# VectorE's side work in attention, spread over five of the eight cycles of a group of heads

## The chip, the cores and the metric

The kernel runs on one core of a Trainium2 chip. Its time is device microseconds per execution, the median of three runs. Times inside an execution come from one profiled execution. The engines are TensorE (PE; its weight loads are PEld), VectorE (DVE), ScalarE (ACT), GpSimd (POOL) and SyncE (SP), which here only issues DMAs.

## The reference

For one sequence of 2048 tokens of width 448, two branches of the same input are mixed by a gate:

```
g = sigmoid((x * gate_w).sum(-1, keepdims=True))
a = attention(x)     # 16 heads of 28, one k and v for all; softmax(q k / sqrt(28)) v, then @ wo
b = x1 + gelu(layernorm(x1) @ w3) @ w4,   x1 = x + shifted(gelu(layernorm(x) @ w1)) @ w2
out = g * a + (1 - g) * b
```

All is computed in float32. The change lies in the attention.

## The kernel before

The projections, the token mixing and the MLP come first (to about 400 us); attention fills the rest. Each product that must be exact is made of three: a tensor is split into a high part, rounded to TensorE's format, and a low part, the rest, and high x high, high x low and low x high are added. The order of instructions on each engine is the order in which the code issues them; no scheduler moves any. Each engine takes its own in that order and waits on semaphores.

Attention runs over 16 groups u (`NU`): four blocks of 512 tokens times four groups of four heads. Within a group, the loop at line 895 makes eight **cycles** i = 0 to 7, each for two tiles of 128 keys. A cycle does this:

- TensorE makes the scores of the first key tile for four heads (`score_tiles`, L203), two heads into single banks, two into a pair of banks. ScalarE takes exponentials from the single banks (L855). VectorE copies the pair to SBUF (L903), and ScalarE takes its exponentials later from there; this spares ScalarE a wait on the banks.
- Then come the second tile's scores, with all exponentials by ScalarE from the banks.
- TensorE multiplies the values by the exponentials of the cycle before (`values`, L866) into a bank that the scores have left, and VectorE adds the result to the group's sum (`values_end`, L788 or L792). This is done in halves of 256 tokens, the first in `s0`, the second in `s1`.
- One **job** of the group before, a product with the output weights (`by_columns`, L818), goes into the other half of the first bank, once the first addition has read it; VectorE adds the result to the output (L837; for the last MLP products, which run as jobs in group 0, L849).

Cycles differ. At i = 2 (`MAX_AT`) the value product is made whole in one bank, and in place of a job TensorE makes a sample of the next group's scores (`max_part`, L210), whose maximum VectorE takes (L212). At i = 5 (`TWICE`) the value product is whole as well, and two jobs run. The jobs of a group are appended at i = 4 of the next one, so that group 0 runs the MLP's and group 1 has none until i = 4.

Beside this, VectorE has **side work**, issued right behind the L903 copy and ahead of `values_end`:

- i = 1: `recip` (L778, L804): the reciprocal of the sums of the group before, which is then sent to memory (`rd`) and read back to all partitions (`rb`, L808).
- i = 3: `max_end` (L236, L237, L240) of the next group, which `later` holds since i = 2: it negates the maximum, splits it and transposes it, and SP issues eight small DMAs (L244) that put it into spare rows of the next group's query `qh`, so that the scores come out with the maximum subtracted. Then `norm` (L813): the sums of the group before times `rb`. Group 0 has no `norm`; group 15 has no next maximum.
- i = 6: `q_begin` (L194, L195), which splits the query of the group after the next (`q_split`) into `qh` and `ql`. Then `q_fetch` has SP load the next raw query into the one buffer `qr` (L189, four DMAs). Groups 14 and 15 have none.

`qh` and `ql` have three buffers each. In group 0, `q_begin(1)` and a fetch stand at i = 1 as well.

Of the kernel before, what the change touches and what calls it, by code (L numbers as in the profile page):

```python
# [10 lines left out]
F32R = mybir.dt.float32r  # L11
# [5 lines left out]
P = 128  # L17
# [19 lines left out]
def f32(ap):  # L37
    return ap.bitcast(F32)
# [3 lines left out]
def gated_mix_kernel(  # L42
# [12 lines left out]
    nc = tc.nc  # L55
# [124 lines left out]
    NU = NB * NG  # L180
    kh_of = []
    qr_of, qh_of, ql_of = {}, {}, {}
# [5 lines left out]
        for j in range(4):  # L188
            nc.sync.dma_start(raw[32 * j:32 * j + DH], qd[g, DH * j:DH * j + DH, 512 * b:512 * b + 512])  # L189

    def q_split(u, qh, ql):
        qr = qr_of.pop(u)
        qh_of[u], ql_of[u] = qh, ql
        nc.vector.tensor_copy(qh, qr)  # L194
        nc.vector.tensor_sub(ql, qr, f32(qh))  # L195

    def scores(u, kt, ps):
        kh = kh_of[0]
# [450 lines left out]
    with tc.tile_pool(name="s2", bufs=1, reuse_waits="tile") as s2, \  # L649
# [36 lines left out]
        for b in range(NB):  # L686
            acc = [ps2.tile([P, 512], F32, tag="acc", bufs=4, name=f"acc_{b}_{t}") for t in range(4)]
            gs = {}
            for f in range(NF):
                if f == 9 and b + 1 < NB:  # L690
                    mv, rs = layernorm_stats(s2a, b + 1)
                if f == 10 and b + 1 < NB:
                    xt4 = big(f"xt4_{b + 1}")[:, 0:4 * D].rearrange("p (f t j) -> p f t j", f=NE, t=4)
                if f in (10, 11) and b + 1 < NB:
                    for t in (2 * f - 20, 2 * f - 19):
                        xn = s2a.tile([P, 512], F32, tag="xn", bufs=1, name=f"xn_{b + 1}_{t}")[:, 0:D]
                        layernorm_norm(b + 1, t, mv, rs, xn, xt4)
                if f == 11 and b + 1 < NB:
                    xt_write(b + 1, xt4)
                    ln_read(b + 1)  # L700
                gs[f] = w3_part(b, f)
                if b == 0 and f % 2 and f < 11:
                    split_w3((f + 3) // 2)
                    split_w4((f + 3) // 2)
                    if f < 9:
                        load_w34((f + 5) // 2, s2)
                if b == 1 and f == 0:
                    nc.gpsimd.tensor_tensor(gg, invE, gz, ALU.pow)
                    nc.vector.tensor_scalar(gg, gg, 1.0, None, op0=ALU.add)
                    nc.vector.reciprocal(gg, gg)  # L710
                    nc.vector.tensor_scalar(gi, gg, -1.0, 1.0, op0=ALU.mult, op1=ALU.add)
                if b == NB - 1 and f == 4:
                    weigh_x1(0, 4 * b)
                if b == 1 and f == 1:
                    nc.gpsimd.memset(f32(khd), 0.0)
                    for j in range(4):
                        h = slice(32 * j, 32 * j + DH)
                        nc.gpsimd.tensor_copy(khd[h, j * MK:(j + 1) * MK], f32(kh_of[0])[h, 0:MK])
                    qr0 = s2a.tile([P, 512], F32, tag="xn", bufs=1, name="qr_0")
                    nc.gpsimd.memset(qr0, 0.0)  # L720
                    q_load(0, qr0)
                    nc.sync.dma_start(w4_late, w4[F - P:F, :])
                if b == 1 and f == 5:
                    q_split(0, qh0, ql0)
                if f >= 2:
                    for t in range(4):
                        w4_part(f - 2, t, gs[f - 2], acc)
                        if b > 1 and t % 2 == 0 and f < NF - 1:
                            fill()
            for t in range(4):  # L730
                w4_part(NF - 2, t, gs[NF - 2], acc, NF - 2 if b == NB - 1 else NF - 1)
                if b + 1 < NB:
                    ln_split(b + 1, t, t + 1)
            for t in range(4):
                if b < NB - 1:
                    w4_part(NF - 1, t, gs[NF - 1], acc)
                xt = x1[:, 4 * b + t, :]
                nc.vector.tensor_add(xt, xt, acc[t][:, 0:D])  # L738
# [5 lines left out]
    with tc.tile_pool(name="s3", bufs=1, reuse_waits="tile") as s3, \  # L744
# [16 lines left out]
        def q_fetch(u):  # L761
            if u < NU:
                q_load(u, qr)

        def q_begin(u):
            q_split(u, s3.tile([P, 512], F32R, tag="qh", bufs=3, name=f"qh_{u}"),
                    s3.tile([P, 512], F32R, tag="ql", bufs=3, name=f"ql_{u}"))

        q_fetch(1)

# [40 lines left out]
        def norm(u, o, rb):  # L811
            on_of[u] = s3.tile([P, 512], F32, tag="on", bufs=2, name=f"on_{u}")
            nc.vector.tensor_mul(on_of[u], o, rb)  # L813
# [81 lines left out]
        for c in range(NC):  # L895
            u, i = divmod(c, NT // 2)
            k = 2 * c
            s0, s1, s2, s3_ = singles if c % 2 == 0 else singles[2:] + singles[:2]
            pa = score_tiles(u, 2 * i, s0, s1, pairs[0])
            exps(pa, left, s0.unsqueeze(1))  # L900
            exps(pa, right, s1.unsqueeze(1))
            if c < NC - 1:
                nc.vector.tensor_copy(pa[:, both], pairs[0])  # L903
            else:
                exps(pa, both, pairs[0])
            while later:
                later.pop(0)()
            if i == 1 and sums:
                norms.append(recip(*sums.pop()))
            if i == 1 and u == 0:  # L910
                q_begin(1)
                q_fetch(2)
            if i == 3 and norms:
                w = norms[0][0]
                norm(*norms.pop())
            if i == 6 and u + 2 < NU:
                q_begin(u + 2)
                q_fetch(u + 3)
            pb = score_tiles(u, 2 * i + 1, s2, s3_, pairs[1])
            exps(pb, left, s2.unsqueeze(1))  # L920
            exps(pb, right, s3_.unsqueeze(1))
            exps(pb, both, pairs[1])
            if c < NC - 1:
                exps(pa, both)
            if i == 4 and u:
                jobs += [(wo_products, wo_add, (u - 1, t), cols) for t in range(4) for cols in halves]
            if c == 0:
                run_jobs(s0, 2)
                run_jobs(s1, 2)
                continue  # L930
            v = (c - 1) // (NT // 2)
            most = 2 if i == TWICE or (u == NU - 1 and i > 3) else 1
            at_max = i == MAX_AT and u + 1 < NU
            if at_max or (most == 2 and jobs):
                values((k - 2, k - 1), s0)
                values_end(v, s0)
                if at_max:
                    max_part(u + 1, range(4), s1)
                    later.append(lambda u=u: max_end(u + 1))
                else:  # L940
                    run_jobs(s1, most)
            else:
                q0, q1 = slice(0, 256), slice(256, 512)
                values((k - 2, k - 1), s0[:, q0], q0)
                values_end(v, s0[:, q0], q0)
                values((k - 2, k - 1), s1[:, q0], q1)
                adds = job_products(s0[:, q1], 1)
                values_end(v, s1[:, q0], q1)
                job_adds(adds)
            if i == 0 and v < NU - 1:  # L950
                sums.append(sums_begin(v))
# [4 lines left out]
        u = NU - 1  # L956
# [84 lines left out]
        with tc.If(again > 0, label="redo"):  # L1041
            for b in range(NB):
                for g in range(NG):
                    u = b * NG + g
                    q_fetch(u)
                    q_begin(u)
                    max_full(u, bank)
                    max_end(u)
                    pv = banks.pop(0)
                    for kt in range(NT):  # L1050
                        ps = [bank(f"s2_{u}_{kt}_{j}") for j in range(4)]
                        scores(u, kt, ps)
                        p = s3.tile([P, 4, 512], F32, tag="p", bufs=PB, name=f"p2_{u}_{kt}")
                        for j in range(4):
                            exps(p, slice(j, j + 1), ps[j].unsqueeze(1))
                        for j in range(4):
                            nc.tensor.matmul(pv[32 * j:32 * j + 32, :], vext[:, kt, :], p[:, j],
                                             start=(kt == 0), stop=(kt == NT - 1), tile_position=(0, 32 * j))
                    values_end(u, pv)
                    banks.append(pv)  # L1060
                    norm(*recip(*sums_begin(u), False))
                    for t in range(4):
                        ps = bank(f"wo2_{u}_{t}")[:, whole]
                        wo_products(u, t, ps)
                        wo_add(u, t, ps)
# [51 lines left out]
```

## Time and profile before

| what | us |
|---|---|
| median of 3 runs (lowest to highest) | 944.64 (944.31 to 945.36) |
| the profiled execution, its own time | 944.86 |
| its span, first to last instruction | 943.1 |
| of that, before the first L903 copy | 403.5 |
| TensorE busy over the span | 928.3 |
| ScalarE busy over the span | 636.9 |
| VectorE busy over the span | 516.7 |

A line of a timeline has the start in us from the span's start, the length, the engine, the line of the code, the operation, what it writes and reads, how many instructions are merged in it, and in brackets how long its engine was idle before it and which instruction ended that. A line of the view by stretch has the bounds, the length, and for each engine the busy time with the number of instructions; then the granted TensorE clock, the DMA engines' share and GB/s. A matmul's end is modelled, so TensorE counted as busy can still be waiting in part. A row of waits has the total time, how often, and the longest.

### The profile page before, as it was taken

The numbers are of one execution on the slowest core, as the hardware profiler recorded it, in microseconds if no ns is written. First come the engines' busy times: TensorE is split into PE (matmuls) and PEld (weight loads), VectorE is DVE, ScalarE is ACT, GpSimd is POOL, SyncE is SP. The second block draws the span as 40 slices with busy tenths as digits, with TensorE's granted clock in tenths as the row PEclk, the third lists the DMA queues.
The fourth block names the chain that finished last, engine by engine and source line by source line (L and its number), as shares of the span: only waits on it lengthen the run. The fifth ranks groups of instructions, "written<-read, shape, count | busy, mean of one in ns | idle before, by whom it ended". The sixth has DMA issues, their size and how long they took to land.

```text
span 943.1 us, 22620 instructions
## 1 busy us (share of the span) xinstructions
PE 928.3 (98%) x9573; PEld 618.1 (66%) x9573; DVE 516.7 (55%) x922; ACT 636.9 (68%) x1006; POOL 81.1 (9%) x111
## 2 busy tenths in 40 slices
PE   9999999999999999999999999999999999999997
PEld 6788888888888888855555555555555555555552
DVE  3665264532432431166666666666666676666664
ACT  5542444332222221289999999999999999999993
POOL 3343420200000520020000000000000000000000
PEclk9999999999999999999999999999999999999998
DMA  9722652210300200020000011000011000010001
GB/s 315 280 76 56 168 164 89 55 48 1 84 1 1 84 1 0 1 62 22 14 15 24 14 42 34 23 13 16 24 43 33 15 23 13 27 41 17 10 14 42
DMA packets 40435, 47.24 MB, mean 50 GB/s; under 512 B 10120, under 2 KB 28488, under 8 KB 40328
## 3 DMA queue, kind: packets, MB, share of 16 engines
q1 hardware_dynamic: 37304, 40.27, 14.5%
q10 hardware_dynamic: 3024, 5.47, 1.6%
q8 instruction: 76, 1.25, 0.6%
q14 instruction: 31, 0.25, 0.1%
HBM read 32.56 MB, written 11.67 MB: 47 GB/s over the span
## 4 chain that ended last, share of the span: by engine, by line
PE 94%; ACT 3%; issue 1%; DMA 0%; DVE 0%; ACTq 0%; DVEq 0%
PE bank L866 25%; PE bank L203 19%; PE bank L818 6%; PE acc L682 5%; PE acc L684 5%; PE acc L683 5%; PE g L135 4%; PE g L136 4%; PE g L137 4%; ACT p L855 3%; PE pair L203 2%; PE hs L460 1%; PE hs L461 1%; PE g L138 1%; PE g L139 1%; PE h L135 1%
## 5 line engine op out<-in xcount | busy, mean ns | idle before, releaser
L855 ACT ACTIVATE p<-bank 128x512 f32<-128x512 f32 x512 | 265.1, 609 | 28.3 <-PE pair L203 18.1
L866 PE MATMUL bank<-p,vext 128*32 128x256 f32 (+1 forms) x3520 | 245.3, 415 | 4.7 <-ACT p L855 1.3
L866 PEld LDWEIGHTS bank<-p,vext 128*32 128x32 f32 x3520 | 101.4, 109 | 125.7 <-ACT p L855 57.5
L903 DVE COPY p<-pair 128x1024 f32<-128x1024 f32 x127 | 155.5, 1225 | 48.8 <-PE pair L203 39.1
L672 ACT ACTIVATE gh<-g 128x512 fp32r<-128x512 f32 x55 | 32.9, 598 | 184.6 <-PE g L139 184.6
L792 DVE TENSOR_TENSOR o<-o,bank 128x256 f32<-128x256 f32 (+1 forms) x188 | 88.1, 469 | 110.2 <-PE bank L866 99.6
L855 ACT ACTIVATE p<-p 128x1024 f32<-128x1024 f32 x127 | 139.5, 1098 | 0.0
L855 ACT ACTIVATE p<-pair 128x1024 f32<-128x1024 f32 x129 | 137.3, 1064 | 0.0
L674 DVE TENSOR_TENSOR gl<-gf,gh 128x512 fp32r<-128x512 f32 x55 | 38.3, 696 | 166.4 <-ACT gf L673 166.4
L203 PE MATMUL bank<-qh,kh 32*128 32x512 f32 x512 | 125.5, 450 | 0.0
L203 PE MATMUL pair<-qh,kh 32*128 32x512 f32 x512 | 118.1, 457 | 0.3 <-DVE x L738 0.3
L203 PE MATMUL bank<-ql,kh 32*128 32x512 f32 x512 | 111.0, 394 | 0.0
L203 PE MATMUL bank<-qh,kl 32*128 32x512 f32 x512 | 108.7, 389 | 0.0
L203 PE MATMUL pair<-qh,kl 32*128 32x512 f32 x512 | 101.0, 388 | 0.0
L203 PE MATMUL pair<-ql,kh 32*128 32x512 f32 x512 | 100.8, 389 | 0.0
L203 PEld LDWEIGHTS bank<-qh,kh 32*128 32x128 f32 x512 | 54.0, 182 | 62.3 <-issue 22.3
L682 PE MATMUL acc<-w4h,gh 128*128 128x448 f32 x220 | 80.3, 365 | 0.0
L684 PE MATMUL acc<-w4h,gl 128*128 128x448 f32 x220 | 80.0, 364 | 0.0
L683 PE MATMUL acc<-w4l,gh 128*128 128x448 f32 x220 | 80.0, 363 | 0.0
L818 PE MATMUL bank<-wof,on 128*32 128x224 f32 (+1 forms) x992 | 68.2, 362 | 0.2
L135 PE MATMUL g<-ah,w3h 128*128 128x512 f32 x168 | 65.8, 392 | 0.0
L136 PE MATMUL g<-al,w3h 128*128 128x512 f32 x168 | 65.7, 391 | 0.0
(199 smaller groups left out, 1416.8 us busy)
## 6 DMA issues: line engine op xcount, KB each, us to landing
qd<-qf ACTq DMA_DIRECT2D x16, 256.0 KB
rb<-rd SPq DMA_DIRECT2D x15, 256.0 KB
x<-in_x_dram SPq DMA_DIRECT2D x4, 896.0 KB
xd<-xt SPq DMA_DIRECT2D x16, 224.0 KB
w34raw<-in_w_dram SPq DMA_DIRECT2D x7, 512.0 KB
qr<-qd SPq DMA_DIRECT2D x64, 56.0 KB
out_dram<-ot SPq DMA_DIRECT2D x15, 224.0 KB
w34raw<-in_w_dram SPq DMA_DIRECT2D x7, 448.0 KB
```

The lines of the kernel that those rows point to most:

```text
L135: nc.tensor.matmul(ps, wh[:, c, :], ah[:, c, :], start=(c == 0), stop=False)
L136: nc.tensor.matmul(ps, wh[:, c, :], al[:, c, :], start=False, stop=False)
L203: nc.tensor.matmul(ps[j], k[h, keys], q[h, :], start=(r == 0), stop=(r == 2), tile_position=(32 * j, 0))
L674: nc.vector.tensor_sub(gl, gf, f32(gh))
L682: nc.tensor.matmul(ps, gh[:, tok], w4h[i][:, k, :], start=(f == 0), stop=False)
L683: nc.tensor.matmul(ps, gh[:, tok], w4l[i][:, k, :], start=False, stop=False)
L684: nc.tensor.matmul(ps, gl[:, tok], w4h[i][:, k, :], start=False, stop=(f == stop))
L792: nc.vector.tensor_add(o, o, pv)
L818: nc.tensor.matmul(ps[32 * i:32 * i + 32, :], a[:, c:c + 32], w, start=True, stop=True, tile_position=(0, 32 * i))
L855: nc.scalar.activation(p[:, heads], p[:, heads] if source is None else source, AF.Exp, scale=SCALE)
L866: nc.tensor.matmul(pv[32 * j:32 * j + 32, :], vext[:, kt, :], p_of[k][:, j, qs], start=(k == ks[0]), stop=(k == ks[-1]), tile_position=(0, ...
L903: nc.vector.tensor_copy(pa[:, both], pairs[0])
```

## The change

`q_split` becomes two functions: `q_high` makes the high part of the query, `q_low` the low part. In the loop the high part is made at i = 5 and the low part, with the fetch behind it, stays at i = 6. `max_end` is taken from `later` at i = 4 instead of at the first chance, which was i = 3. Where a split stood whole elsewhere (in the MLP, at i = 1 of group 0, and in the fallback that runs when a check of the sums fails) both functions are called one after the other. So the side work of a group, which stood in cycles 1, 3 and 6, stands in 1, 3, 4, 5 and 6. The number of instructions of each engine is the same, and so is the order on TensorE, ScalarE and GpSimd; VectorE's order changes, and on SP the DMAs of `max_end` move with it, in groups 4, 8 and 12 past the DMA of one output row.

```diff
-    def q_split(u, qh, ql):
-        qr = qr_of.pop(u)
+    def q_high(u, qh, ql):
         qh_of[u], ql_of[u] = qh, ql
-        nc.vector.tensor_copy(qh, qr)
-        nc.vector.tensor_sub(ql, qr, f32(qh))
+        nc.vector.tensor_copy(qh, qr_of[u])
+
+    def q_low(u):
+        nc.vector.tensor_sub(ql_of[u], qr_of.pop(u), f32(qh_of[u]))
...
         def q_begin(u):
-            q_split(u, s3.tile([P, 512], F32R, tag="qh", bufs=3, name=f"qh_{u}"),
-                    s3.tile([P, 512], F32R, tag="ql", bufs=3, name=f"ql_{u}"))
+            q_high(u, s3.tile([P, 512], F32R, tag="qh", bufs=3, name=f"qh_{u}"),
+                   s3.tile([P, 512], F32R, tag="ql", bufs=3, name=f"ql_{u}"))
...
-            while later:
+            if i == 4 and later:
                 later.pop(0)()
             if i == 1 and sums:
                 norms.append(recip(*sums.pop()))
             if i == 1 and u == 0:
                 q_begin(1)
+                q_low(1)
                 q_fetch(2)
             if i == 3 and norms:
                 w = norms[0][0]
                 norm(*norms.pop())
+            if i == 5 and u + 2 < NU:
+                q_begin(u + 2)
             if i == 6 and u + 2 < NU:
-                q_begin(u + 2)
+                q_low(u + 2)
                 q_fetch(u + 3)
```

More of the change, by code (lines that the diff above doesn't have):

```diff
@@ L723, in gated_mix_kernel @@
                 if b == 1 and f == 5:
-                    q_split(0, qh0, ql0)
+                    q_high(0, qh0, ql0)
+                    q_low(0)
                 if f >= 2:
@@ L1046, in gated_mix_kernel @@
                     q_begin(u)
+                    q_low(u)
                     max_full(u, bank)
```

## The prediction

> **What bounds the kernel now.** I read four views: the page for the whole run, the busy time of each engine by stretch, the waits of ScalarE, and the instructions in order of time, for one group after another. The page ends the question of a share of busy time at once: TensorE is busy nearly always, so the share alone says nothing of where a microsecond can be won.
>
> ```profile
> PE 928.3 (98%) x9573; PEld 618.1 (66%) x9573; DVE 516.7 (55%) x922; ACT 636.9 (68%) x1006; POOL 81.1 (9%) x111
> ```
>
> The change lies in attention alone. The second view gives 470 to 895 us, thirteen whole groups of heads (u = 2 to 14) of eight cycles each; the third gives ScalarE's waits in the same stretch (columns: total us, times, longest).
>
> ```profile
> 470.00:895.00 425.00, 421.76 (x6260) 222.77 (x6256) 284.64 (x504) 405.26 (x620) 0.00 (x0) 1.00 0.08 24
> ```
>
> ```profile
> ACT p L855 <- PE pair L203: 15.7, 47, 0.4
> ACT p L855 <- PE bank L203: 2.6, 8, 0.4
> ```
>
> ScalarE works 405.3 of 425.0 us and waits 18.3 us, 55 times, always for score products. That is just over four waits in each of 13 groups. Where they sit, the time order of ScalarE in group u = 6 shows (start, us, engine and line, idle before it in brackets); the first instruction of a cycle is the one on a bank:
>
> ```profile
> 611.36 2.06 ACT L855 ACTIVATE p<-bank 128x512 f32<-128x512 f32 x4 [0.23 <-PE pair L203]
> ...
> 615.67 2.07 ACT L855 ACTIVATE p<-bank 128x512 f32<-128x512 f32 x4 [0.39 <-PE pair L203]
> ...
> 623.94 2.06 ACT L855 ACTIVATE p<-bank 128x512 f32<-128x512 f32 x4 [0.40 <-PE pair L203]
> ...
> 628.20 2.06 ACT L855 ACTIVATE p<-bank 128x512 f32<-128x512 f32 x4 [0.34 <-PE bank L203]
> ```
>
> I name a cycle c0 to c7 by its i, and let it run from one L903 copy to the next. ScalarE's idle 0.39 us closes c3, 0.40 closes c5, 0.34 closes c6; the 0.23 behind c2 is not touched. 13 x (0.23 + 0.39 + 0.40 + 0.34) = 17.7 of the 18.3 us; the other 0.6 stand in three c1, where the reciprocal waited for its DMA:
>
> ```profile
> DVE good L778 <- DMA rt<-o: 2.0, 3, 0.7
> ```
> VectorE in the same cycles:
>
> ```profile
> 611.38 1.22 DVE L903 COPY p<-pair 128x1024 f32<-128x1024 f32 x1 [0.18 <-PE pair L203]
> 612.52 0.16 DVE L236 TENSOR_SCALAR mc<-mr 128x16 fp32r<-128x16 f32 x1
> ...
> 613.07 0.65 DVE L813 TENSOR_TENSOR on<-o,rb 128x512 f32<-128x512 f32 x1
> 613.63 0.42 DVE L792 TENSOR_TENSOR o<-o,bank 128x256 f32<-128x256 f32 x1
> ...
> 615.69 1.22 DVE L903 COPY p<-pair 128x1024 f32<-128x1024 f32 x1 [0.48 <-PE pair L203]
> 617.52 0.42 DVE L792 TENSOR_TENSOR o<-o,bank 128x256 f32<-128x256 f32 x1 [0.60 <-PE bank L866]
> ...
> 619.64 1.22 DVE L903 COPY p<-pair 128x1024 f32<-128x1024 f32 x1 [0.47 <-PE pair L203]
> 622.32 0.69 DVE L792 TENSOR_TENSOR o<-o,bank 128x512 f32<-128x512 f32 x1 [1.46 <-PE bank L866]
> ...
> 623.95 1.23 DVE L903 COPY p<-pair 128x1024 f32<-128x1024 f32 x1
> 625.10 0.42 DVE L194 CAST qh<-qr 128x512 fp32r<-128x512 f32 x1
> 625.55 0.69 DVE L195 TENSOR_TENSOR ql<-qr,qh 128x512 fp32r<-128x512 f32 x1
> 626.16 0.41 DVE L792 TENSOR_TENSOR o<-o,bank 128x256 f32<-128x256 f32 x1
> ...
> 628.22 1.23 DVE L903 COPY p<-pair 128x1024 f32<-128x1024 f32 x1 [0.48 <-PE bank L203]
> ```
>
> The reader is to see three lengths. c4, which has no side work, takes 615.69 to 619.64, 3.95 us, and in it VectorE idles 0.60 us ahead of the first L792 addition. c3 takes 4.31 us, c6 4.27 us, and in both VectorE goes from the copy through side work into L792 with no idle time. L792 frees the bank into which TensorE writes the next output product (L818), and behind that stand the scores of the next cycle, on which ScalarE waits. So **the loop of TensorE, VectorE and ScalarE** bounds the stage; side work costs time once it is longer than the cover of 0.60 us behind the copy.
>
> **How much of the two stalls is VectorE's.** Not all of it, and TensorE shows why. These rows are its value products in c3 and in c4:
>
> ```profile
> 612.15 1.93 PE L866 MATMUL bank<-p,vext 128*32 128x256 f32 x32
> ```
>
> ```profile
> 616.33 1.93 PE L866 MATMUL bank<-p,vext 128*32 128x256 f32 x32
> ```
>
> In c4 they start 0.64 us behind the copy, in c3 0.77 us: TensorE itself comes late out of c2, where the scores waited for the reduce. In c4 the first L792 follows 1.19 us (617.52 less 616.33) behind the value products; in c3 that would be 613.34, only 0.29 us ahead of the 613.63 measured. The cycle can't fall back to 3.95 us. Two cycles of the trace show what is left when side work is missing. In group u = 0 there is no norm, so c3 holds max_end alone; in group u = 14 there is no query to split, so c6 holds nothing:
>
> ```profile
> 416.17 1.22 DVE L903 COPY p<-pair 128x1024 f32<-128x1024 f32 x1 [0.18 <-PE pair L203]
> ...
> 418.15 0.42 DVE L792 TENSOR_TENSOR o<-o,bank 128x256 f32<-128x256 f32 x1 [0.22 <-PE bank L866]
> ...
> 420.26 1.22 DVE L903 COPY p<-pair 128x1024 f32<-128x1024 f32 x1 [0.46 <-PE pair L203]
> ```
>
> ```profile
> 887.09 1.23 DVE L903 COPY p<-pair 128x1024 f32<-128x1024 f32 x1
> 889.18 0.42 DVE L792 TENSOR_TENSOR o<-o,bank 128x256 f32<-128x256 f32 x1 [0.86 <-ACT p L855]
> ...
> 891.30 1.23 DVE L903 COPY p<-pair 128x1024 f32<-128x1024 f32 x1 [0.46 <-PE pair L203]
> ```
>
> So c3 is 4.09 us with 0.55 us of side work, VectorE then waiting 0.22 us for TensorE; c6 is 4.21 us with none.
>
> **The change part by part.**
>
> *max_end leaves c3.* Its three instructions fill 612.52 to 613.07, 0.55 us. The norm (0.65 us) then starts at 612.52 and ends at 613.17, ahead of the 613.34 at which TensorE lets the first L792 go. VectorE is no longer last, as in group 0, and c3 goes from 4.31 to 4.09: **0.22 us saved**. TensorE's late start is what is last then.
>
> *max_end enters c4.* The copy there begins at 615.69; the next instruction can start 1.14 us later (611.38 to 612.52), at 616.83, and 0.55 us of work ends at 617.38, ahead of the L792 at 617.52. The idle 0.60 us hides it with 0.14 us to spare: cost 0. Its input, the maximum of c2, is then a whole cycle old. With no cover it would cost 0.55 us in each group. Nothing else waits in line but L792, and L818 behind it.
>
> *The query's high half moves from c6 to c5.* It takes 0.42 us, and c5 has 1.46 us of idle time ahead of its only L792, since there all value products come first: cost 0, or 0.42 us without that cover. c5's own 0.40 us stays; it has two output products, and TensorE alone sets it. The raw query was loaded behind c6 of the group before, so no wait is added.
>
> *c6 keeps the low half.* 0.69 us from 625.10 ends at 625.79. In group 14 the first L792 came 2.09 us behind the copy, here 626.04, so VectorE isn't last: c6 goes from 4.27 towards 4.21, **0.06 us saved**.
>
> *The DMAs.* max_end issues eight small DMAs on SP, and with it they move one cycle back. The norm reads rb, and now starts 0.55 us earlier.
>
> ```profile
> 606.20 0.54 SPq L808 DMA_DIRECT2D rb<-rd  x1
> 613.21 4.56 SPq L244 DMA_DIRECT2D qh<-mrow  x8
> ```
>
> The issues would run from about 617.5 to 622.1. SP's next work, the loads of the next query, follows the low half, at 625.79 or later, so nothing queues behind them. In groups 4, 8 and 12 the output row of c3 is issued ahead of them instead of behind. The rows that they write are read by the next group's first scores, after c7's copy at 628.22, 6 us later. rb has been issued 5.8 us before the norm's new start. I cost both at 0.
>
> *How many groups.* c3 has both pieces and an output product in u = 2 to 14, 13 groups. In u = 1 the output products have not begun, and ScalarE opens c4 there with no idle time, so nothing is to be had:
>
> ```profile
> 451.30 1.12 ACT L855 ACTIVATE p<-bank 128x512 f32<-128x512 f32 x2
> ```
>
> c6 has the split and an output product in u = 1 to 13, 13 groups.
>
> **The sum.** 13 x 0.22 + 13 x 0.06 = 2.86 + 0.78 = 3.64 us, say 3.6. The profiled execution took 944.86 us (span 943.1 and 1.8 around it), which would be 941.3. It lies 0.2 above the median of the runs, 944.64; from that the forecast is **941.0 us**. Bounds of what the trace does not show: c4's margin of 0.14 us is small, and a loss of 0.05 in each of the 15 groups that have a max_end takes 0.8 back; the side work of c6 may cost all of its 0.06 still, 0.8 less; the 0.6 us of ScalarE's waits behind late reciprocals may go or double. That is 2.0 to 4.2 us, or 940.4 to 942.6, with 0.4 for the runs' own spread below.
>
> **The rivals.**
>
> *The stalls aren't VectorE's (no change, 944.6).* If TensorE's lag alone made c3 and c6 long, moving side work would do nothing. For it: the lag is real, and c6 without side work is only 0.06 us shorter. Against it: L792 has no idle time before it in c3 and has 0.22 us of it in group 0. [...] Chance 8%.
>
> *c4 pays in part (943.1).* If c3's extra 0.14 us in group 0 (4.09 less 3.95) were max_end's price and not the lag's, c4 would take it on in each of the 15 groups that have a max_end (u = 0 to 14): 15 x 0.14 = 2.1 us of the 3.6 given back. Against it is the 0.22 us of idle time behind max_end in group 0. Chance 5%.
>
> *Both stalls go whole (935.8).* c3 and c6 at 3.95 us would save 13 x (0.36 + 0.32) = 8.8 us. The two rows of groups 0 and 14 speak against it. Chance 4%.
>
> *Slower: max_end is exposed in c4 (949.2).* The first output product of a new set is issued in c4, behind L792. If there L792 could start as soon as VectorE is free, all 0.55 us would delay L792, L818, the scores and ScalarE: 15 x 0.55 = 8.2 us, less the 3.6 saved, is 4.6 us slower. It decides from a delay of 0.24 us in each c4 on, where cost and gain are equal (3.6 / 15); for that the cover of 0.60 us would have to shrink to some 0.3. It doesn't in c4 of group 6, where the copy before it is as long and TensorE's value products begin 0.64 us behind it. Chance 4%.
>
> **How the numbers follow.** Forecast 79%, no change 8%, c4 in part 5%, both whole 4%, slower 4%. Runs of this kernel tell 0.2% (1.9 us) from no change, so faster is below 942.75: forecast and both whole, 0.83; within 0.2%: no change and c4 in part, 0.13; slower 0.04. The range takes the forecast's bounds and the near end of the second rival: 940.0 to 942.9.
>
> **What would show it.** In the profile of the changed kernel the L903 copies should stand 4.09 us apart in c3, 3.95 in c4, 4.31 in c5 as before, 4.21 in c6; idle time of about 0.2 us ahead of L792 in c3 and c6 and about 0.1 in c4; ScalarE's idle time about 0.17 behind c3 and 0.29 behind c6, and its waits in the 13 groups about 14.7 us instead of 18.3. An L792 in c4 without idle time, or a copy there later than 3.95 us, would be the second or the last rival. A stall in front of the norm would show that rb lands later than I take it to.

## The result, and the profile after

The changed kernel takes **940.44 us** (median of 6 runs, 939.28 to 941.63), the kernel before 944.95 us beside it (6 runs, 942.69 to 945.37). The ratio is 0.9961, with an interval of 0.9951 to 0.9971; it is an estimate from all the runs, not the quotient of the two medians (0.9952), and is worth 3.7 us. On the 944.64 us of the prediction that is 940.96 us. The profiled execution of the changed kernel took 941.63 us; its span is 939.8 us, 3.3 us under that of before (3.23 by the unrounded times, which the sums below use).

First the page's line of busy times, and the view by stretch for the same thirteen groups (u = 2 to 14), which now end at 891.9 us:

```profile
PE 924.7 (98%) x9573; PEld 618.8 (66%) x9573; DVE 516.5 (55%) x922; ACT 637.4 (68%) x1006; POOL 81.6 (9%) x111
```

```profile
470.00:891.90 421.90, 418.65 (x6260) 223.66 (x6256) 284.39 (x504) 405.73 (x620) 0.00 (x0) 1.00 0.08 24
```

VectorE and ScalarE do the same work as before, to within 0.5 us; what went is waiting. TensorE's busy time falls from 421.76 to 418.65 us with the same 6260 matmuls, so part of what the profile counts as busy was waiting. ScalarE's waits in that stretch (total us, times, longest):

```profile
ACT p L857 <- PE pair L204: 11.0, 42, 0.5
ACT p L857 <- PE bank L204: 3.9, 13, 0.4
```

They sum to 14.9 us instead of 18.3, in as many places (55). Where they shrank, ScalarE's order of time in group 6 shows; these rows open c4 and c7, and the bracket is the idle time left by the cycle before:

```profile
614.35 2.06 ACT L857 ACTIVATE p<-bank 128x512 f32<-128x512 f32 x4 [0.17 <-PE bank L204]
...
626.83 2.06 ACT L857 ACTIVATE p<-bank 128x512 f32<-128x512 f32 x4 [0.30 <-PE pair L204]
```

Behind c3 0.17 instead of 0.39, behind c6 0.30 instead of 0.34; behind c2 and c5 the 0.23 and 0.39 us stand as they were. VectorE in the same group, c3 to c6:

```profile
610.28 1.23 DVE L905 COPY p<-pair 128x1024 f32<-128x1024 f32 x1 [0.17 <-PE bank L204]
611.42 0.68 DVE L815 TENSOR_TENSOR on<-o,rb 128x512 f32<-128x512 f32 x1
612.25 0.42 DVE L794 TENSOR_TENSOR o<-o,bank 128x256 f32<-128x256 f32 x1
...
614.37 1.22 DVE L905 COPY p<-pair 128x1024 f32<-128x1024 f32 x1 [0.46 <-PE bank L204]
...
615.92 0.21 DVE L241 STREAM_TRANSPOSE mrow<-mc 128x32 f32<-128x32 f32 x1
616.21 0.42 DVE L794 TENSOR_TENSOR o<-o,bank 128x256 f32<-128x256 f32 x1
...
618.32 1.22 DVE L905 COPY p<-pair 128x1024 f32<-128x1024 f32 x1 [0.46 <-PE pair L204]
619.46 0.42 DVE L193 CAST qh<-qr 128x512 fp32r<-128x512 f32 x1
621.00 0.69 DVE L794 TENSOR_TENSOR o<-o,bank 128x512 f32<-128x512 f32 x1 [1.12 <-ACT p L857]
...
622.63 1.22 DVE L905 COPY p<-pair 128x1024 f32<-128x1024 f32 x1
623.77 0.68 DVE L196 TENSOR_TENSOR ql<-qr,qh 128x512 fp32r<-128x512 f32 x1
624.72 0.42 DVE L794 TENSOR_TENSOR o<-o,bank 128x256 f32<-128x256 f32 x1 [0.27 <-ACT p L857]
...
626.85 1.23 DVE L905 COPY p<-pair 128x1024 f32<-128x1024 f32 x1 [0.46 <-PE pair L204]
```

From copy to copy: c3 614.37 less 610.28 is 4.09 us (4.31 before), c4 3.95 (3.95), c5 4.31 (4.31), c6 4.22 (4.27). In c3 and c6, where VectorE ran from the copy through its side work into the addition, it now idles 0.15 us (610.28 to 612.25: the norm ends at 612.10) and 0.27 us ahead of it. In c4 max_end ends at 616.13 and the addition starts at 616.21.

The copies of all groups, compared between the two profiles, divide the 3.23 us:

| where | us |
|---|---|
| c3 in u = 2 to 14 | -2.91 (0.224 each) |
| c6 in the 11 groups u = 2 to 13 other than 9 | -0.54 (0.049 each) |
| c5 and c6 of group 9 | +0.29 (+0.21 and +0.075) |
| c1 of group 0, where VectorE waits for the query's DMA | +0.38 |
| the other cycles (c6 of u = 1 is -0.045 of it) | -0.07 |
| ahead of the first copy, and behind attention | -0.34, -0.04 |

The part ahead of the first copy, which the change doesn't touch, took 401.25 to 403.7 us in the profiles of this study, and c1 of group 0 took 5.13 to 5.85 us. Each kernel was profiled once, so it isn't shown how much they differ between runs of one kernel; but the 45 runs of the kernel before in this study spread over 3.7 us (941.95 to 945.69), and these two parts would account for most of that. So below I read the spacing of copies inside attention first, and the time of the runs second.

### The profile page after: what moved, and what is told of

Same layout as the page of the kernel before. It is cut to its first block, busy times and chain, and to the rows that moved or that the text cites. A ratio compares the mean times of both kernels' runs of the same rounds, so it can differ in the third digit from the quotient of the medians.

```text
span 939.8 us, 22620 instructions
## 1 busy us (share of the span) xinstructions
PE 924.7 (98%) x9573; PEld 618.8 (66%) x9573; DVE 516.5 (55%) x922; ACT 637.4 (68%) x1006; POOL 81.6 (9%) x111
## 4 chain that ended last, share of the span: by engine, by line
PE 92%; ACT 4%; DMA 1%; issue 1%; DVE 1%; SPq 0%; POOL 0%; ACTq 0%; DVEq 0%
PE bank L868 24%; PE bank L204 18%; PE bank L820 5%; PE acc L683 5%; PE acc L685 5%; PE acc L684 5%; ACT p L857 4%; PE g L135 4%; PE g L136 4%; PE g L137 4%; PE pair L204 2%; PE hs L461 1%; PE hs L462 1%; PE g L138 1%; PE g L139 1%; PE h L135 1%
```

## The experiments

The first theory is the prediction's: VectorE's side work costs time only from the point at which the cycle's first addition becomes late, and c3's rest, 4.09 instead of 3.95 us, is TensorE's late start out of c2. The rivals: the parts of the change trade with each other (max_end or the split pays where it went), or the lag isn't what holds c3. Cycle lengths are medians of groups 2 to 14 in us; c0, c1 and c7 are 3.95 in all kernels. "Attention" is the change of all cycles together against the profile of before; it holds c1 of group 0, which by itself differs by up to 0.55 us. "13 groups" is the change in u = 2 to 14 alone. The ratio is estimated from the runs as above.

| kernel | c2 | c3 | c4 | c5 | c6 | 13 groups | attention | median of the runs | ratio, interval |
|---|---|---|---|---|---|---|---|---|---|
| before | 4.15 | 4.31 | 3.95 | 4.32 | 4.26 | | | | |
| after | 4.15 | 4.09 | 3.95 | 4.32 | 4.21 | -3.21 | -2.85 | 940.44 | 0.9961, 0.9951 to 0.9971 |
| max_end alone moved | 4.15 | 4.08 | 3.95 | 4.32 | 4.26 | -2.86 | -2.59 | 942.21 | 0.9979, 0.9969 to 0.9990 |
| split alone moved | 4.15 | 4.31 | 3.95 | 4.32 | 4.21 | -0.20 | -0.06 | 944.26 | 1.0002, 0.9991 to 1.0013 |
| max_end and high half both in c4 | 4.15 | 4.09 | 4.13 | 4.32 | 4.21 | -0.94 | -0.66 | 943.40 | 0.9995, 0.9982 to 1.0007 |
| after, sample of 16 keys | 4.12 | 3.95 | 3.95 | 4.31 | 4.21 | -5.40 | -5.64 | 938.82 | 0.9937, 0.9920 to 0.9953 |
| before, sample of 16 keys | 4.12 | 4.31 | 3.95 | 4.31 | 4.26 | -0.38 | -0.05 | 943.06 | 0.9989, 0.9979 to 1.0000 |
| after, double job in c4 | 4.15 | 4.09 | 4.31 | 4.09 | 3.95 | -4.58 | -4.56 | 939.43 | 0.9952, 0.9934 to 0.9970 |
| both of these | 4.12 | 3.95 | 4.31 | 4.09 | 3.95 | -6.84 | -7.07 | 935.86 | 0.9909, 0.9893 to 0.9926 |

The kernel before had a median of 943.46 us beside the three in which a part was moved, and 944.55 us beside the last four.

### One part at a time

max_end alone moves to c4; the split stays whole in c6:

```diff
-            if i == 5 and u + 2 < NU:
-                q_begin(u + 2)
             if i == 6 and u + 2 < NU:
+                q_begin(u + 2)
                 q_low(u + 2)
```

> Of the change, only the move of max_end from c3 to c4; the query is split whole in c6, as before. My theory (side work costs what it has over the room behind the copy): c3 4.09 us, c4 3.95, c5 4.31, c6 4.26 as before, so 13 x 0.22 = 2.9 us less than before, some 941.7 to 942.0. Rival 'c4 pays in part': c4 4.0 to 4.1 and 1 to 2 us less gain. Rival 'the stalls are not VectorE's': c3 stays at 4.31 and the time at that of before.

c3's gain came whole with this part: 2.94 us in 13 groups, and c6 stayed. In group 6 the copy of c3 stands at 610.73, the norm at 611.87, the addition at 612.70 and the next copy at 614.82: the same steps as in the changed kernel, 4.09 us in all.

The split alone; max_end stays in c3:

```diff
-            if i == 4 and later:
+            if i == 3 and later:
```

> Of the change, only the query's high half in c5; max_end is back in c3 with the norm. My theory: c3 4.31 us as before, c5 4.31 (1.46 us of idle time hide 0.42), c6 4.21, so 13 x 0.05 = 0.7 us less than before, hardly to be told from no change by time, but plain in the spacing of the copies. If VectorE alone made c6 long, c6 would fall to 3.95 and the gain would be 4 us. If c5's cover is not there, c5 is 4.73 and the kernel 5 us slower.

c6 fell by 0.53 us in all, group 9 included (0.46 in the changed kernel). But c5 of group 9 grew by 0.21 us, and c1 by 0.15 in the groups where the reciprocal's DMA is late; with 0.18 in c1 of group 0 nothing was left (-0.06), and the runs show no difference (1.0002). So **the gain is max_end's**, and the split is worth about 0.3 us net. That rests on the copies. The runs alone give max_end 0.21% and the whole change 0.39%, with intervals that just overlap, and the two were not run beside each other.

### Both pieces in c4

```diff
-            if i == 5 and u + 2 < NU:
+            if i == 4 and u + 2 < NU:
                 q_begin(u + 2)
```

> As the changed kernel, but the query's high half stands in c4 beside max_end, and c5 has no side work. In c4 VectorE then has 0.55 + 0.42 us of work and some 0.03 between, 1.00 us, where the room from the earliest start behind the copy (1.14 us) to the first addition (1.83 us) is 0.69 us. My theory: c4 becomes 3.95 + 0.31 = 4.26 us in u = 0 to 13, all else as in the changed kernel, so about 4.2 us slower than the changed kernel and about the time of before. [...]

c4 grew, and 2.22 of the 2.92 us won in c3 were given back:

```profile
613.90 1.22 DVE L905 COPY p<-pair 128x1024 f32<-128x1024 f32 x1 [0.45 <-PE pair L204]
...
615.63 0.43 DVE L193 CAST qh<-qr 128x512 fp32r<-128x512 f32 x1
615.97 0.41 DVE L794 TENSOR_TENSOR o<-o,bank 128x256 f32<-128x256 f32 x1
...
618.03 1.22 DVE L905 COPY p<-pair 128x1024 f32<-128x1024 f32 x1 [0.49 <-PE pair L204]
```

The idle time ahead of the addition is gone, and it starts 2.07 us behind the copy instead of 1.84; the cycle takes 4.13 us instead of 3.95 (4.06 in groups 5, 9 and 13, where the addition starts at 2.00; 4.38 in group 7, at 2.32). The sign is as expected, the size (0.18 for 0.31) is not, for two reasons. The addition was expected at 1.14 + 1.00 = 2.14 us and started at 2.07: 615.63 to 615.97 shows that it starts 0.09 us before the cast is counted as ended, so the durations sum to more than they take. And it came 0.24 us later than the 1.83 us of a free addition, of which only 0.18 was paid; the dose below shows the missing 0.06. This is the last rival's mechanism, made to happen.

### The dose

To measure the room behind the copy, idle subtractions of growing width are put there, one width in each group: rising with the group in c3, falling in c7, larger in c5, there behind the cast of the high half (group 14 has no cast). The rest of the kernel stays as it is.

```diff
+            if u in DOSE.get(i, {}):
+                for n in DOSE[i][u]:
+                    nc.vector.tensor_sub(spare[:, 0:n], gf_late[:, 0:n], gf_late[:, 0:n])
             pb = score_tiles(u, 2 * i + 1, s2, s3_, pairs[1])
```

> The changed kernel with idle subtractions added to VectorE's side work in groups 2 to 14: in c3 from 16 columns (about 0.17 us) rising to 512 and then 512 + 256 columns (0.69 and about 1.1 us), in c7 the same falling, in c5 from 512 columns (0.69 us) to 512 + 512 + 256 (about 1.8 us). Only the lengths of these cycles by dose are read; the total time says nothing. My theory: a cycle grows by what the side work has over its room, one for one: in c7 (room 0.69 us, no other work) nothing up to a dose of 0.69 us, then up to +0.4; in c3 (room 0.83 us because TensorE is late, of which the norm takes 0.65) nothing up to 0.18 us, then up to +0.9; in c5 (room 1.54 us, of which the high half takes 0.42) nothing up to 1.12 us, then up to +0.7. Rival without rooms: each cycle grows by its dose from the first. Rival 'not VectorE's': nothing grows.

Two doses in c7, in groups 4 (512 columns) and 2 (512 and 256):

```profile
559.53 1.23 DVE L911 COPY p<-pair 128x1024 f32<-128x1024 f32 x1 [0.46 <-PE pair L204]
560.67 0.68 DVE L932 TENSOR_TENSOR spare<-gf_late 128x512 f32<-128x512 f32 x1
561.36 0.42 DVE L794 TENSOR_TENSOR o<-o,bank 128x256 f32<-128x256 f32 x1
...
563.48 1.23 DVE L911 COPY p<-pair 128x1024 f32<-128x1024 f32 x1 [0.47 <-PE pair L204]
```

```profile
494.07 1.23 DVE L911 COPY p<-pair 128x1024 f32<-128x1024 f32 x1 [0.46 <-PE pair L204]
495.21 1.14 DVE L932 TENSOR_TENSOR spare<-gf_late 128x512 f32<-128x512 f32 x2
496.27 0.93 DVE L794 TENSOR_TENSOR o<-o,bank 128x256 f32<-128x256 f32 x2
...
498.33 1.23 DVE L911 COPY p<-pair 128x1024 f32<-128x1024 f32 x1 [0.49 <-PE pair L204]
```

0.68 us of work costs nothing (563.48 less 559.53 is 3.95), 1.14 us costs 0.31 (4.26); 256 and 256 columns, in group 3, put the addition at 1.94 us behind the copy and cost 0.05 (4.00). The same in c3, on top of the norm, with 512 and 256 columns in group 14:

```profile
871.05 1.23 DVE L911 COPY p<-pair 128x1024 f32<-128x1024 f32 x1 [0.18 <-PE bank L204]
...
873.86 0.74 DVE L794 TENSOR_TENSOR o<-o,bank 128x256 f32<-128x256 f32 x2
...
875.92 1.23 DVE L911 COPY p<-pair 128x1024 f32<-128x1024 f32 x1 [0.49 <-PE pair L204]
```

The addition starts 2.81 us behind the copy and the cycle takes 4.87. Through all doses that are paid in c3 and c7 runs one line, to 0.02 us: **cycle = start of the first addition behind the copy + 2.06 us** (2.08 gives 4.13, 2.34 gives 4.40, 2.81 gives 4.87); before's c3 lies on it (2.25, 4.31) and so does the c4 with two pieces (2.07, 4.13). Below it the cycle is TensorE's: 3.95, or 4.09 in c3. The columns of c3's doses:

| columns | 16 to 192 | 256 | 320 | 384 | 448 | 512 | 256+256 | 512+256 |
|---|---|---|---|---|---|---|---|---|
| c3, us | 4.09 | 4.13 | 4.20 | 4.29 | 4.35 | 4.40 | 4.60 | 4.87 |

In c7 all doses up to 512 columns left 3.95. Side work can start 1.14 us behind the copy. Until it makes the addition late it has 0.69 us of room in c4 and c7 (the free additions start at 1.83) and 0.83 us in c3 (at 1.97). The cycle grows only 0.06 us after that: the line meets 3.95 at 1.89 and 4.09 at 2.03. In group 7 of the changed kernel max_end ended late by itself, and the c4 addition started at 1.91 us without idle time; the cycle took 3.95 all the same.

In c5 the free addition starts at 2.68 us. Two doses of 512 columns behind the cast, 1.33 us of work, put it at 2.80 and cost nothing, where some 0.2 was expected. A third dose of 128 columns, in group 13, put it at 3.13 and cost 0.13 in c5 and 0.14 in the c6 behind it. In group 14, without the cast, 1280 columns put it at 2.93 and cost 0.02 and 0.06. So in these three groups c5 and c6 together grow by what the addition starts later than some 2.85 us. That is 0.17 us more room than the free start shows. A reason may be that this cycle's jobs are made in another bank than the one that the addition reads; no run tests that.

### TensorE's lag out of c2

The sample of the next group's scores, made in c2, sets when TensorE comes to c3. It is halved, in both kernels; the maximum that is subtracted then comes from 16 keys instead of 32.

```diff
-MK = 32
+MK = 16
```

> The changed kernel with a sample of 16 keys instead of 32 for the maximum that is subtracted (the softmax is the same for any subtracted value within range). Theory: TensorE's lag, which kept c3 at 4.09 us, comes from c2, where the sample's products stand ahead of the next scores and the 0.69 us reduce holds a bank that the second tile's scores need. With half the sample the reduce takes 0.42 us and the products about half: c2 falls from 4.15 to about 3.95 and c3 from 4.09 to about 3.95 (norm alone, 0.65 us, fits in the 0.69 us of room), some 0.34 us in each of 13 groups, 4.4 us less than the changed kernel, about 936.5. Rival: c3's last 0.14 us is VectorE's (norm), then c3 stays at 4.09 and only c2 gains, 2.6 us.

> The kernel before with the sample of 16 keys, to see what the change is worth where TensorE comes without lag. Theory: max_end and norm together still put the first addition at 2.25 us behind the copy, and a cycle ends 2.06 us behind its first addition, so c3 stays at 4.31 us while c2 falls to 3.95. Against the run with 16 keys and the change, c3 would then differ by 0.36 us instead of 0.22, and the change would be worth 13 x 0.36 + 13 x 0.05 = 5.3 us instead of 3.6. Rival (c3's stall is TensorE's): c3 falls with the lag, to about 4.17, and the change stays worth 3.6 or less.

With the change, c3 fell to 3.95 us, as low as a cycle without any lag:

```profile
609.55 1.22 DVE L905 COPY p<-pair 128x1024 f32<-128x1024 f32 x1 [0.42 <-PE pair L204]
...
611.38 0.42 DVE L794 TENSOR_TENSOR o<-o,bank 128x256 f32<-128x256 f32 x1
...
613.50 1.22 DVE L905 COPY p<-pair 128x1024 f32<-128x1024 f32 x1 [0.46 <-PE pair L204]
```

The copy now waits 0.42 us (0.17 before), and the addition starts at 1.83 us. In the kernel before, with max_end and norm both in c3, the same edit wins nothing there:

```profile
610.55 1.23 DVE L903 COPY p<-pair 128x1024 f32<-128x1024 f32 x1 [0.42 <-PE pair L203]
...
612.80 0.87 DVE L792 TENSOR_TENSOR o<-o,bank 128x256 f32<-128x256 f32 x2
...
614.86 1.23 DVE L903 COPY p<-pair 128x1024 f32<-128x1024 f32 x1 [0.49 <-PE pair L203]
```

The addition starts at 2.25 us and c3 stays 4.31. That tells the theory from the rival: c3 ends with whichever is later, TensorE's lag or VectorE's side work, and with the lag gone the change is worth 0.36 us a group in c3 instead of 0.22. c2 missed its expectation: 4.12 us, where 3.95 was expected. What sets c2 beside the sample is open.

Which part of the sample makes the lag, the waits of TensorE's weight loads show. In both kernels with 32 keys they wait for the reduce (L212 before, L213 after) once in each of the 13 groups:

```profile
PEld bank L203 <- DVE mr L212: 2.5, 13, 0.2
```

With 16 keys the reduce takes 0.42 us instead of 0.69 and this row is missing from both profiles; the value products of c3 then start 0.63 us behind the copy instead of 0.77. So the lag out of c2 is TensorE waiting for a bank that VectorE's reduce still reads.

### The double job in c4

By the same law c5's 4.32 and c6's 4.21 us should be the price of c5's whole value product and two jobs, and of the lag that they leave to c6. Here the two come in c4, the two jobs as one product of 448 columns:

```diff
-        TWICE = 5
+        TWICE = 4
...
-                part = ps[:, 0:D // 2] if n == 1 else ps[:, cols]
+                part = ps[:, 0:cols.stop - cols.start] if n == 1 else ps[:, cols]
...
-                jobs += [(wo_products, wo_add, (u - 1, t), cols) for t in range(4) for cols in halves]
+                jobs += [(wo_products, wo_add, (u - 1, t), cols) for t in range(4) for cols in ([whole] if t == 0 else halves)]
...
-                    run_jobs(s1, most)
+                    run_jobs(s1, 1 if jobs[0][3] is whole else most)
```

> The changed kernel with the double job in c4 instead of c5, taken as one product of 448 columns with one addition, so that VectorE's tail is 0.68 us instead of 0.81 and max_end stands in a cycle whose only addition comes late. Theory: c5's old 4.31 us moves to c4 and stays about 4.31 (TensorE's product time is the same); the cycle behind it, now c5, is 4.21 less the 0.13 us by which the bank is freed earlier, about 4.08, and c6 is 3.95 with the low half just inside its room. 13 x 0.13 = 1.7 us less than the changed kernel, about 939. Rival: the cycle behind the double job is set by TensorE's product time, then 4.21 stays and nothing is gained.

```profile
612.37 1.23 DVE L905 COPY p<-pair 128x1024 f32<-128x1024 f32 x1 [0.46 <-PE bank L204]
...
616.68 1.23 DVE L905 COPY p<-pair 128x1024 f32<-128x1024 f32 x1 [0.18 <-PE bank L204]
...
620.76 1.23 DVE L905 COPY p<-pair 128x1024 f32<-128x1024 f32 x1 [0.46 <-PE pair L204]
...
624.71 1.23 DVE L905 COPY p<-pair 128x1024 f32<-128x1024 f32 x1 [0.47 <-PE pair L204]
```

c4 takes 4.31 us, the next cycle 4.09 (copy's wait 0.18, as in c3 behind c2), and c6 is 3.95 with the low half in it (its copy at 620.76, the next at 624.71). c4 to c6 take 12.35 us instead of 12.48. This tells the theory from the rival: in group 6 TensorE's weight loads wait 0.31 us for the output additions of the double job in the changed kernel (at 622.63) and 0.19 us here (at 616.55), and the cycle behind the job fell by the same 0.12 us. The edit moves the double job and merges it at once; what the move alone would win is not shown. In groups 3 and 5 late starts of the kind of group 9 below cost 0.31 us in c1 and 0.23 in c4. Both edits together:

> The changed kernel with both, 16 sample keys and the double job as one of 448 columns in c4. Theory: the two gains add, c2 and c3 3.95, c4 4.31, c5 4.08, c6 3.95; some 6 us less than the changed kernel, about 935. If one lag feeds the other they add to less.

They add, as expected: beyond the change the two edits win 2.20 and 1.37 us in the 13 groups alone, and 3.63 together. Attention is 7.07 us shorter than before, and **935.86 us** (934.72 to 936.84) is the fastest kernel of the study, faster than before and after.

### Group 9

In the changed kernel c5 of group 9 took 4.53 us and the c6 behind it 4.35; in the other groups c5 was 4.32. On VectorE:

```profile
716.22 1.23 DVE L905 COPY p<-pair 128x1024 f32<-128x1024 f32 x1 [0.45 <-PE pair L204]
...
718.90 0.69 DVE L794 TENSOR_TENSOR o<-o,bank 128x512 f32<-128x512 f32 x1 [1.12 <-ACT p L857]
720.02 0.81 DVE L839 SCALAR_TENSOR_TENSOR ot<-bank,gg,x 128x224 f32<-128x224 f32 x2 [0.44 <-PE bank L820]
720.75 1.22 DVE L905 COPY p<-pair 128x1024 f32<-128x1024 f32 x1
```

In the kernel before, the output addition of that cycle follows the value addition at once:

```profile
721.01 0.69 DVE L792 TENSOR_TENSOR o<-o,bank 128x512 f32<-128x512 f32 x1 [1.46 <-PE bank L866]
721.78 0.81 DVE L837 SCALAR_TENSOR_TENSOR ot<-bank,gg,x 128x224 f32<-128x224 f32 x2
```

The late start is 0.44 us of idle time instead of 0.08, for data that had been ready: the wait ahead of it had ended at 719.63. Counting from 0 every instruction that VectorE's trace shows, its semaphore waits too, those that start so much late for no visible reason in the traces of this study are numbers 575, 703, 831, 959, 1087 and 1215: all 63 modulo 128. In the kernel before, number 959 is the copy that opens c6, which shows no delay. In the changed kernel the high half's cast and the wait issued with it stand ahead of c5's additions, and number 959 is the first of the two output additions. The cast itself isn't the cause: with the high half in c4, c5 of group 9 has no cast and took 4.53 us too, and with the split whole in c6 it took 4.32. To test the count, two idle instructions are put at the start of the changed kernel and of the kernel before. What was number 957 is then 959: in the changed kernel the value addition of c5, which has 1.12 us of idle time ahead, in the kernel before the first output addition. If the delay belongs to the addition itself, nothing changes:

```diff
     nc.vector.memset(warm, 0.0)
+    for i in range(2):
+        nc.vector.memset(keep.tile([P, 4], F32, name=f"pad_{i}"), 0.0)
```

> The changed kernel with two idle VectorE memsets of 4 columns in front of everything, to test what made c5 and c6 of group 9 long (4.53 and 4.35 us instead of 4.31 and 4.21, in each kernel with the high half ahead of that point). [...]

> The kernel before with the same two memsets. [...]

The same cycle in the changed kernel and in the kernel before, each with the two instructions:

```profile
714.49 1.23 DVE L907 COPY p<-pair 128x1024 f32<-128x1024 f32 x1 [0.47 <-PE bank L206]
...
717.52 0.69 DVE L796 TENSOR_TENSOR o<-o,bank 128x512 f32<-128x512 f32 x1 [1.47 <-ACT p L859]
...
718.85 1.21 DVE L907 COPY p<-pair 128x1024 f32<-128x1024 f32 x1
```

```profile
718.44 1.23 DVE L905 COPY p<-pair 128x1024 f32<-128x1024 f32 x1 [0.47 <-PE pair L205]
...
722.24 0.81 DVE L839 SCALAR_TENSOR_TENSOR ot<-bank,gg,x 128x224 f32<-128x224 f32 x2 [0.43 <-PE bank L820]
722.97 1.21 DVE L905 COPY p<-pair 128x1024 f32<-128x1024 f32 x1
```

The delay moved two instructions up in both. In the kernel before it now sits ahead of its output addition and c5 of group 9 is 4.53 us, as in the changed kernel. In the changed kernel it sits ahead of the value addition (idle 1.47 us instead of 1.12), where it is borne in part: c5 took 4.36, and the c6 behind it 4.36 too, where 4.32 and 4.21 are usual. The two together are 8.71 us, where 8.88 stood without the two instructions and 8.53 is usual: half of the delay of 0.35 us was paid still. The addition was at 3.03 us, 0.18 behind the 2.85 of the dose. These two kernels ran once each (939.77 and 945.41 us, beside 944.1 for the kernel before), which says nothing finer than the cycles do.

## Why the prediction was right

**What bounds the stage.** The loop of TensorE, VectorE and ScalarE, as put: side work inside the room costs nothing, and beyond it the cycle grows one for one with the start of the first addition. The room in c4 was put at 0.55 + 0.14 = 0.69 us; the doses give 0.69 until the addition is late, and 0.06 more until the cycle grows. The 0.60 us of idle time that the prediction first calls the cover is less than the room, since side work can start 0.08 us before the copy is counted as ended. Its share of busy time, taken by itself, would have left VectorE alone: it is busy 284.39 of 421.90 us, 67%, where ScalarE is at 96%. The order of VectorE's work took 2.9 us out of attention all the same. A share of busy time doesn't see which work stands ahead of an instruction that others wait for.

**max_end out of c3.** 0.22 us in each of 13 groups was forecast, 0.224 came. The floor was named rightly: the norm ends 0.15 us before the addition, and with half the sample c3 drops to 3.95 us. The reduce ahead of it sets that floor, as the prediction had it.

**max_end into c4.** Forecast 0, measured 0: c4 is 3.95 us in the changed kernel. The margin was a little smaller than worked out, 0.08 us of idle time for 0.14. Two pieces in c4 show the price without the cover, 0.18 us a group.

**High half in c5.** No cost by its work, as forecast; 1.33 us of doses behind it were free as well. What wasn't foreseen is group 9: two instructions more ahead of c5's additions brought number 959 onto one of them, for 0.29 us. That the change paid for it is chance: it hangs on a count.

**Low half in c6.** The term of the sum that was mis-sized: 0.06 us x 13 = 0.78 was taken, 0.049 x 12 = 0.59 measured (u = 1 to 13 without 9). The 4.27 of group 6 stood for a median of 4.26. With group 9 the split's part of the change is 0.30 us, not 0.78.

**The DMAs** cost nothing: the norm starts 1.14 us behind the copy, as soon as VectorE is free, so `rb` had landed, and no later group's c0 grew.

**The sum.** 3.64 us was forecast; the terms that the change owns gave 2.91 + 0.59 - 0.29 = 3.21. Group 0's c1 took 0.38 back and the part ahead of the first copy gave 0.34, neither of them by the change as far as the spread of those parts among all profiles shows. The runs give 3.7 us by the ratio and 4.5 by the medians; the difference from the 3.2 us of the profile lies within their own spread (939.28 to 941.63, and 942.69 to 945.37). So the mechanism was right, and that 940.96 us falls on the forecast of 941.0 to 0.04 is luck: the change's own terms came out 0.4 us short, and the rest is spread. The lower bound of the gain, 2.0 us, also leaves out the 0.6 us that is said may double; with it the bound is 1.4 us, or 943.2.

**The other rivals.** "c4 pays in part" fell with c4's 3.95 us. "Both stalls go whole" fell with c3's 4.09; once the lags go as well, with two edits more than the change, c3 and c6 both take 3.95 us. That the time is then 935.86 us, about the 935.8 that this rival named, is chance: attention is 7.07 us shorter, not 8.8, since c4 grew by more than c5 and c2 fell. "Slower" would have needed c4's room to be some 0.3 us; it is 0.69.

## What to carry to other kernels

Where engines hand work around in a loop, find the one instruction on the side engine that others wait for, measure how far behind its predecessor it would start with nothing between (here 0.69 us of room, and 0.06 more that didn't lengthen the cycle), and fill each cycle up to that and no further. A piece taken out of an overfull cycle pays only down to the next late thing, so look up what that is before counting the whole stall (c3: 0.22 of 0.36 us). Where the next late thing is a lag from the cycle before, shortening that cycle's work and moving side work pay more together than apart: in the 13 groups 0.38 us for the shorter sample alone, 3.21 for the move alone, 5.40 for both.

## What the runs showed of the hardware

**Instructions of VectorE that stand 128 apart started late.** The late ones in attention have numbers that are 63 modulo 128. In the changed kernel number 831 had 0.22 us and number 959 0.36 us more idle time ahead than the same instruction in other groups, and with two instructions more ahead the delay in group 9 moved by two (idle 1.47 us instead of 1.12 in the changed kernel, 0.43 instead of 0.08 in the kernel before). The page's list of queues has one whose packets start near these places (packets, MB, share):

```profile
q14 instruction: 31, 0.25, 0.1%
```

In the profiles of the kernels before and after, one of these packets starts within 1.5 us of each of the six numbers named with group 9. But in group 9 of the changed kernel it starts at 720.70 us, 0.68 us behind the late addition at 720.02, so the addition didn't wait for it. What the addition waits for isn't shown. What the delay cost depended on the instruction it fell on: nothing where number 959 was the copy that opens c6, 0.29 us where it was an output addition, for whose bank the next scores wait. For a change of a few tenths of a us this is an effect of its own.

**Independent instructions of VectorE overlapped at their ends.** The copy is 1.22 us long and the next starts 1.14 us behind its start; behind a norm of 0.68 us the dose starts after 0.60. A queue of such pieces took about 0.08 us less for each than the sum of durations, which is part of why the two pieces in c4 cost 0.18 us where 0.31 was expected. Two pieces that write the same tile showed no such overlap: the doses of 0.68 and 0.42 us in c7 took 1.14 together.
